# Seven-product blocks in the first layer, another order of blocks, and shifted due times in a planned attention and two-layer kernel

## The chip, the core and the metric

The kernel runs on one core of a Trainium2 chip. Five engines work side by side: PE (TensorE, matrix products), PEld (its weight loads, which overlap PE), DVE (VectorE), ACT (ScalarE), POOL (GpSimd), and SP, whose queue issues all DMAs. The metric is the device time of one execution in microseconds; less is better. What a measurement of this kernel can tell from no change is about 0.2%, some 2.2 us.

## The reference

Attention over 4 batches, 8 heads, 768 positions and 64 columns, with a mask of global and local keys and a bias by distance; its output, 3072 tokens of 512 columns, goes through two layers one after the other.

```
scores = scale * q @ k.T + bias ; masked by keep
a = exp(scores - max) ; a = a / (sum(a) + 1e-9)
x = a @ v                       # 3072 tokens x 512
h = x @ w_in ; g = h * cos(h) ; y = g @ w_out            # first layer, d_ff = 2048
h = max(y @ w_in2, 0) ; out = (h * h) @ w_out2           # second layer
```

## The kernel before

**Blocks.** The tokens are cut into 24 tiles T of 128, and these into six blocks of 512 tokens. Attention runs by tile, in two groups of four heads (`attend`, `group`; `attend32` and `group32` for the first four tiles). Each block then passes through the first layer (m = 0) and the second layer (m = 1). The list SEQ gives the order of these twelve stages.

**Numbers in two parts.** A matrix product in full precision is made as three products of fp16 parts: each operand is split into a high part (an ACT copy) and a low part (a subtraction, `split_lo`, on DVE or on POOL). A unit of the first layer (`first`, 128 hidden columns) is 12 matmuls of 512 columns into one bank of PSUM; `hidden` computes g from it (two ACT steps, a DVE step on line 1099, and a split), and three units later `second` makes another 12 matmuls of 512 columns.

**Weights.** They come as 64-bit numbers. `decoded` turns a pair of rows into fp32 with one ACT step (line 56) and three DVE steps (lines 62, 65, 68), and `weight` splits the result. Sixteen pairs serve the first layer. The tiles w_0 to w_7 keep the eight of the first product; the others go to `ld` tiles, and from there to DRAM and back for each block. The sixteen decodings, the attention of block 0 and that of block 1 all lie ahead of the first layer of block 0 or beside it: this stretch is called the ramp here.

**Seven products.** A product of two 2 x 2 block matrices can be made from seven block products in place of eight. The second layer does its first half so in all six blocks (`four_blocks`, matmuls of 256 columns on line 1166), and its second half so in the blocks named by TWO (`second2`, line 1302); other blocks use `tokens` (line 1372, 512 columns). The code for seven products in the first layer is there too (`four_sums`, `quarters_of_pair`, `four_blocks1`, `second_quarter`), for the blocks named by SEVEN, which is empty.

**Order.** Nothing is issued in the order written. Each step is added to `Plan` with a due time, the engines that may run it and its duration as the planner assumes it; `Plan.order` walks through time and, engine by engine, gives the free engine the ready step with the earliest due time. POOL takes a split when DVE is busy. Buffers come from small pools (4 banks `h`, 4 banks `yp`, 8 tiles `t`, 3 tiles `v`, 2 tiles `e`, 2 `dec`, 2 `raw`). The due times come from `nominal` (attention) and `unit_due` (units and weights).

**Lengths.** `lengths_of_x` runs 16 small matmuls (line 1499) for each block, for a check of the largest argument of the cosine.

## Time and profile before

| | us |
|---|---|
| median of 3 runs | 1114.02 (1113.53 to 1114.48) |
| the profiled execution, device time | 1113.74 |
| its span in the trace | 1112.0 |
| PE busy | 1077.9 |
| DVE busy | 738.1 |
| ACT busy | 734.9 |
| POOL busy | 159.2 |

The trace is of one execution, 0.28 us under the median; its span leaves 1.74 us outside. A matmul's modelled length overlaps the next one's, so the cadence of matmuls is read from start to start, or as a full window divided by its count. A group of matmuls that follow each other without a gap is one row of the timeline.

### The profile page before, as it was taken

Reading aid. Unit: us, or ns where it says so; the run is one execution under the profiler, and the core shown is the slowest. Engines: PE = TensorE matmul, PEld = TensorE weight load, DVE = VectorE, ACT = ScalarE, POOL = GpSimd, SP = SyncE. Lnnn points to the kernel's source line nnn. Section 1 sums busy time; section 2 is a strip of 40 time slices with the busy share of each in tenths; the row PEclk is TensorE's granted clock in tenths of the full one; section 3 lists DMA queues with packets and bytes.
Section 4 is the critical chain, followed back from the end, with each engine's and each line's share of the span. In section 5 each row is a group of like instructions: output and inputs, shape, how many; then the busy total and the mean of one; then the engine's idle time right before and its main releaser. Section 6 shows DMA issues by size and latency. Waiting matters only on the chain.

```text
span 1112.0 us, 21314 instructions
## 1 busy us (share of the span) xinstructions
PE 1077.9 (97%) x8612; PEld 676.5 (61%) x8612; DVE 738.1 (66%) x1341; ACT 734.9 (66%) x1279; POOL 159.2 (14%) x131
## 2 busy tenths in 40 slices
PE   6898889999999999999999999999999999999997
PEld 5744445554455444666666554666544588888886
DVE  6998996668877895675544563455684278477473
ACT  7988867788987664866654865674554277367360
POOL 0210322121130110110000110000140033023010
PEclk9989989999999999999999999999999999999999
DMA  5578778649779773786876624586874363334201
GB/s 218 192 218 209 240 241 251 167 101 274 219 164 226 307 256 127 246 256 211 258 201 221 188 80 94 143 222 187 334 255 148 112 230 131 126 132 153 86 2 42
DMA packets 151979, 207.65 MB, mean 187 GB/s; under 512 B 103808, under 2 KB 104320, under 8 KB 150336
## 3 DMA queue, kind: packets, MB, share of 16 engines
q1 hardware_dynamic: 151872, 206.21, 60.3%
q8 instruction: 69, 1.13, 0.4%
q14 instruction: 38, 0.31, 0.1%
HBM read 149.03 MB, written 32.51 MB: 163 GB/s over the span
## 4 chain that ended last, share of the span: by engine, by line
PE 93%; DVE 5%; ACT 1%; DMA 1%; issue 0%; SPq 0%; DVEq 0%; ACTq 0%
PE hps L1059 22%; PE ypps L1075 22%; PE hps L1166 20%; PE ypps L1372 11%; PE ypps L1302 8%; PE hps L925 2%; PE hps L864 2%; PE hps L1302 2%; PE ypps L761 1%; DVE dec L65 1%; PE hps L879 1%; PE hps L733 1%; PE hps L1499 1%; PE hps L813 1%; DVE dec L68 1%; DMA ld<-kq 1%
## 5 line engine op out<-in xcount | busy, mean ns | idle before, releaser
L1059 PE MATMUL hps<-xy,w 128*128 128x512 f16 x1152 | 269.7, 386 | 9.2 <-DVE w L422 4.8
L1075 PE MATMUL ypps<-g,ld 128*128 128x512 f16 x1152 | 263.7, 379 | 0.4 <-issue 0.4
L1166 PEld LDWEIGHTS <-ld 128*128 128x128 f16 x2016 | 196.2, 98 | 32.3 <-issue 0.7
L1059 PEld LDWEIGHTS <-w 128*128 128x128 f16 x1152 | 111.8, 99 | 144.7 <-issue 11.7
L1166 PE MATMUL hps<-ys,ld 128*128 128x256 f16 x1680 | 196.1, 273 | 0.0
L1075 PEld LDWEIGHTS <-ld 128*128 128x128 f16 x1152 | 111.4, 98 | 131.2 <-issue 0.7
L422 DVE TENSOR_TENSOR g<-t,g 128x512 f16<-128x512 f32 x138 | 103.2, 748 | 53.5 <-ACT g L1143 52.9
L1360 DVE TENSOR_TENSOR t<-hps,t 128x512 f32<-128x512 f32 x120 | 82.7, 689 | 83.6 <-PE hps L1166 82.2
L1372 PE MATMUL ypps<-ld,g 128*128 128x512 f16 x576 | 133.7, 379 | 0.0
L1099 DVE SCALAR_TENSOR_TENSOR t<-t,hps 128x512 f32<-128x512 f32 x96 | 65.6, 684 | 83.8 <-ACT t L1097 83.7
L1095 ACT ACTIVATE t<-hps 128x512 f32<-128x512 f32 x96 | 57.0, 594 | 88.1 <-PE hps L1059 85.4
L1143 ACT ACTIVATE g<-t 128x512 f16<-128x512 f32 x144 | 90.0, 625 | 35.8 <-DVE t L1099 34.5
L1372 PEld LDWEIGHTS <-g 128*128 128x128 f16 x576 | 55.7, 98 | 57.0
L1357 ACT ACTIVATE t<-t 128x512 f32<-128x512 f32 x72 | 45.0, 625 | 55.9 <-DVE t L1360 55.8
L422 POOL TENSOR_TENSOR p<-e,p 128x1024 f16<-128x1024 f32 (+1 forms) x14 | 28.2, 2015 | 239.6 <-ACT p L912 207.6
L1097 ACT ACTIVATE t<-t 128x512 f32<-128x512 f32 x96 | 60.4, 629 | 2.6
L1192 ACT ACTIVATE t<-t 128x512 f32<-128x512 f32 x96 | 60.2, 628 | 2.6
L1357 ACT ACTIVATE t<-hps 128x512 f32<-128x512 f32 x24 | 14.3, 595 | 52.8 <-PE hps L1166 52.8
L888 DVE CUSTOM_DVE_ANT_0 e<-hps,bias 128x256 f32<-128x256 f32 (+2 forms) x96 | 31.7, 386 | 21.0 <-PE hps L864 20.7
L65 DVE SCALAR_TENSOR_TENSOR dec<-raw,dec 128x1024 int32<-128x1024 int32 x32 | 43.7, 1367 | 0.6
L422 DVE TENSOR_TENSOR p<-e,p 128x1024 f16<-128x1024 f32 (+1 forms) x26 | 30.2, 1160 | 20.6 <-ACT p L912 18.9
L422 POOL TENSOR_TENSOR g<-t,g 128x512 f16<-128x512 f32 x18 | 23.2, 1292 | 138.3 <-ACT g L1143 112.7
(195 smaller groups left out, 1527.1 us busy)
## 6 DMA issues: line engine op xcount, KB each, us to landing
ld<-w SPq DMA_DIRECT2D x146, 512.0 KB, 4.2
raw<-w SPq DMA_DIRECT2D x32, 1024.0 KB, 5.5
w<-ld SPq DMA_DIRECT2D x36, 512.0 KB, 3.3
ld<-kq SPq DMA_DIRECT2D x23, 512.0 KB, 5.6
ld<-vt SPq DMA_DIRECT2D x24, 256.0 KB, 4.3
yd<-xy SPq DMA_DIRECT2D x6, 1024.0 KB, 5.8
xy<-yd SPq DMA_DIRECT2D x6, 1024.0 KB, 5.7
ld<-w SPq DMA_DIRECT2D x24, 256.0 KB, 3.7
```

Of the source, the lines that this page charges most:

```text
L422: op.emit = lambda: eng[op.eng].tensor_tensor(out=out_f(), in0=src_f(), in1=hi_f(), op=ALU.subtract)
L1059: nc.tensor.matmul(out=at(ps), lhsT=w_view(wt)[:, a, j % 2, k * 128:(k + 1) * 128], rhs=x_view(src)[:, c, k, :], start=(n == 0), stop=(n = ...
L1075: nc.tensor.matmul(out=at(y_ps[d]), lhsT=wv[:, a, d * 128:(d + 1) * 128], rhs=at(g)[:, c], start=(j == 0 and n == 0), stop=(j == NJ - 1 an ...
L1097: act(due + 1.2, 512, lambda: nc.scalar.activation(out=at(t), in_=at(t), func=ACTF.Square, scale=HALF_TURN), w=[t])
L1099: dve(due + 1.9, 0.7, lambda: nc.vector.scalar_tensor_tensor(out=at(t), in0=at(t), scalar=-S_X / S_H, in1=at(ps), op0=ALU.add, op1=ALU.mul ...
L1143: act(due, 512, lambda: nc.scalar.activation(out=at(g)[:, 0], in_=at(t), func=ACTF.Copy), r=[t], new=[g])
L1166: nc.tensor.matmul(out=at(bank)[:, 256 * u:256 * u + 256], lhsT=wv(a, u, kk), rhs=sv(c, kk), start=(fresh and u == n == 0), stop=(last and ...
L1192: act(due, 512, lambda: nc.scalar.activation(out=at(t), in_=at(t), func=ACTF.Square), w=[t])
L1302: nc.tensor.matmul(out=at(bank)[:, 256 * half:256 * half + 256], lhsT=gv(home)[:, z, c0:c0 + 128], rhs=wv(a, u), start=(q == half == u == ...
L1357: act(due, 512, lambda: nc.scalar.activation(out=at(t), in_=at(ps), func=ACTF.Relu, scale=ROOT), **k)
L1360: dve(due, 0.7, lambda: nc.vector.tensor_tensor(out=at(t), in0=at(bank), in1=at(u), op=ALU.add), port=False, **k)
L1372: nc.tensor.matmul(out=at(y_ps[d]), lhsT=at(g)[:, z, 256 * u + d % 2 * 128:256 * u + d % 2 * 128 + 128], rhs=wv[:, a, u], start=(q == i == ...
```

## The change

The stages stand in another order (block 5's first layer ahead of block 2's second), and block 5's attention is due 30 us sooner. Blocks 4 and 5 now use seven products in the first layer, and block 2 joins the blocks with seven products in the last half of the second layer. The matmuls of `lengths_of_x` are kept for blocks 0 and 1; for the others an ACT square with a running sum takes their place. The due times of attention steps ("P", "A", "X" with the tile) and of the first layer's weights ("W") are shifted by a table of 43 numbers. Where the planner sees PE idle before 240 us of its own time, `idle_products` and `spin` put matmuls of a zero tile on PE. Some temporary tiles come from other pools (`e` for `dec`, `t` for `v`).

```diff
+SHIFTS = {
+    ('A', 0, 0): 7.9,
...
+    ('W', 1, 7): -24.7,
...
+EARLY = 30.0
...
+SPIN_FROM = 0.9
+SPIN_PART = 0.75
+SPIN_UNTIL = 240.0
...
     def order(self):
 
+        for o in self.work:
+            o.due += SHIFTS.get(o.tag, 0.0)
...
-    SEQ = [(0, 0), (0, 1), (0, 2), (0, 3), (1, 0), (1, 1), (0, 4), (1, 2), (0, 5), (1, 3), (1, 4), (1, 5)]
+    SEQ = [(0, 0), (0, 1), (0, 2), (0, 3), (1, 0), (1, 1), (0, 4), (0, 5), (1, 2), (1, 3), (1, 4), (1, 5)]
...
+        if b == NB - 1:
+            s0, s1 = s0 - EARLY, s1 - EARLY
...
-    SEVEN = ()
+    SEVEN = (4, 5)
...
-        if b in SEVEN:
+        if b > 1:
             sq = new("t")
             measured.append(act(s + 24, 600, lambda: nc.scalar.activation(
                 out=at(sq), in_=at(x32), func=ACTF.Square, accum_out=norms[:, T:T + 1]), r=[x32], new=[sq]))
+        if b in SEVEN:
             pair.append(x32)
...
-    TWO = (3, 4, 5)
+    TWO = (2, 3, 4, 5)
...
-        up, low = new("dec"), new("dec")
+        up, low = new("e"), new("e")
...
-            tiles[b, n] = tuple(new("v") for _ in range(3))
+            tiles[b, n] = tuple(new("t" if (b, n) == (TWO[-1], 1) else "v") for _ in range(3))
...
-        if m == 0 and b not in SEVEN:
+        if m == 0 and b < 2:
             lengths_of_x(b, start[0, b] + 6)
...
+            if last is not None and o.start < SPIN_UNTIL and biased[0].end < o.start:
+                gap = o.start - last.end
+                open_y = [y for y in sums.values() if y[1].end <= last.end]
+                if gap > SPIN_FROM:
...
+                    n = int(SPIN_PART * (o.start - begin) / 0.216)
+                    if bank is not None and n > 0:
+                        out[o] = bank, n, not open_y
...
+    def spin(bank, n, fresh):
+
+        for _ in range(n):
+            nc.tensor.matmul(
+                out=at(bank), lhsT=nought, rhs=bias.rearrange("p h c -> p (h c)")[:, 0:512], start=fresh, stop=fresh,
+                skip_group_check=True)
+
     order = plan.order()
+    idle = idle_products(order)
     with tc.manual_schedule():
         for o in order:
+            if o in idle:
+                spin(*idle[o])
             o.emit()
```

**First place: DVE in the ramp, up to the split of w_4**, the weight tile that the ninth unit needs. raw and dec are the tiles of a weight that is being decoded, x_1 and g_125 belong to attention's output, nm to attention's row maxima, t and hps to a unit's `hidden`. Before:

```order
L65 SCALAR_TENSOR_TENSOR dec_105<-raw_64,dec_105 128x1024
L68 SCALAR_TENSOR_TENSOR dec_105<-raw_64,dec_105 128x1024
L62 TENSOR_SCALAR dec_104<-dec_104 128x1024
L941 RECIPROCAL sm_93<-sm_93 128x4
L942 TENSOR_TENSOR x_1_123<-hps_133,sm_93 128x2x128
L65 SCALAR_TENSOR_TENSOR dec_104<-raw_63,dec_104 128x1024
L820 TENSOR_REDUCE nm_87<-hps_135 128x2
L820 TENSOR_REDUCE nm_87<-hps_136 128x2
L824 TENSOR_SCALAR nm_87<-nm_87 128x4
L422 TENSOR_TENSOR g_125<-x_1_123,g_125 128x512
L68 SCALAR_TENSOR_TENSOR dec_104<-raw_63,dec_104 128x1024
L422 TENSOR_TENSOR w_4_110<-dec_105,w_4_110 128x1024
```

After, the same place:

```order
L62 TENSOR_SCALAR dec_105<-dec_105 128x1024
L65 SCALAR_TENSOR_TENSOR dec_105<-raw_64,dec_105 128x1024
L1165 SCALAR_TENSOR_TENSOR t_116<-t_116,hps_136 128x512
L68 SCALAR_TENSOR_TENSOR dec_105<-raw_64,dec_105 128x1024
L1165 SCALAR_TENSOR_TENSOR t_117<-t_117,hps_135 128x512
L703 SCALAR_TENSOR_TENSOR v_82<-ld_70,v_82 128x8x64
L474 TENSOR_TENSOR w_4_110<-dec_105,w_4_110 128x1024
```

Attention's maxima and the next weight's steps no longer stand between w_4's decoding and its split: 147 instructions stand ahead of that split before, 128 now (and one of these is a new memset). The sixteenth unit's step on line 1099 (1165 now) has 208 ahead of it before and 206 now.

**Second place: DVE just ahead of the first unit**, whose operand is the split of xy_101 into xy_102. Before:

```order
L422 TENSOR_TENSOR p_97<-e_95,p_97 128x1024
L65 SCALAR_TENSOR_TENSOR dec_105<-raw_64,dec_105 128x1024
L68 SCALAR_TENSOR_TENSOR dec_105<-raw_64,dec_105 128x1024
L422 TENSOR_TENSOR ld_69<-dec_104,ld_69 128x1024
L422 TENSOR_TENSOR xy_102<-xy_101,xy_102 128x1024 x2
```

After:

```order
L474 TENSOR_TENSOR ld_72<-dec_105,ld_72 128x1024
L68 SCALAR_TENSOR_TENSOR dec_104<-raw_63,dec_104 128x1024
L703 SCALAR_TENSOR_TENSOR v_83<-ld_67,v_83 128x8x64
L474 TENSOR_TENSOR xy_102<-xy_101,xy_102 128x1024
L878 TENSOR_REDUCE nm_88<-hps_133 128x2
L878 TENSOR_REDUCE nm_88<-hps_134 128x2
```

One half of the operand's split stays on DVE and the other moves to POOL, and a third attention group's maxima (nm_88) follow at once.

**Third place: DVE in the second layer of block 1**, where a bank of PSUM is freed by the sums on line 1360 (1426 now). Before:

```order
L1360 TENSOR_TENSOR t_118<-hps_135,t_119 128x512
L1360 TENSOR_TENSOR t_119<-hps_134,t_119 128x512
L422 TENSOR_TENSOR g_125<-t_118,g_125 128x512
L941 RECIPROCAL sm_91<-sm_91 128x4
L942 TENSOR_TENSOR x_0_122<-hps_133,sm_91 128x2x128
L1360 TENSOR_TENSOR t_115<-hps_134,t_115 128x512
```

After:

```order
L1426 TENSOR_TENSOR t_121<-hps_136,t_121 128x512
L474 TENSOR_TENSOR g_128<-t_117,g_128 128x512
L631 TENSOR_TENSOR t_114<-dec_104,dec_105 128x512
L631 TENSOR_TENSOR dec_105<-dec_105 128x2x256
L474 TENSOR_TENSOR g_124<-t_118,g_124 128x512
L631 TENSOR_TENSOR t_115<-dec_105,dec_104 128x512
L474 TENSOR_TENSOR g_127<-t_121,g_127 128x512
L1426 TENSOR_TENSOR t_117<-hps_135,t_117 128x512
L652 TENSOR_TENSOR dec_104<-w_3_109 128x1024
```

The sums of weights for the first layer's seven products (`four_sums`, lines 631 and 652) now stand between the sums that free PE's banks. In all, the planned path has 1442 DVE instructions for 1341 before, 62 more on ACT and 62 more on POOL; of the sums on line 1360 there are 160 for 120.

## Rows read from the trace of the kernel before

**Rows 1.** The page: span, part 1 (busy time), PEclk of part 2.

```profile
span 1112.0 us, 21314 instructions
PE 1077.9 (97%) x8612; PEld 676.5 (61%) x8612; DVE 738.1 (66%) x1341; ACT 734.9 (66%) x1279; POOL 159.2 (14%) x131
PEclk9989989999999999999999999999999999999999
```

**Rows 2.** Waits of PE: waiter, releaser, total us, times, longest.

```profile
PE hps L1059 <- DVE w L422: 4.8, 2, 3.0
PE hps L813 <- ACT e L828: 4.7, 2, 2.5
...
PE hps L1059 <- DVE dec L68: 1.9, 1, 1.9
...
PE hps L1166 <- DVE t L1360: 0.5, 1, 0.5
```

**Rows 3.** Timeline of PE, ramp: start, length, instruction, count, idle before and releaser.

```profile
59.56 4.41 PE L1059 MATMUL hps<-xy,w 128*128 128x512 f16 x11 [0.97 <-DVE xy L422]
63.80 1.06 PE L1499 MATMUL hps<-xy 128*128 128x128 f16 x16
64.69 2.75 PE L1059 MATMUL hps<-xy,w 128*128 128x512 f16 x12
67.28 0.89 PE L925 MATMUL hps<-v,pt 128*128 128x65 f16 x24
...
109.22 4.92 PE L1059 MATMUL hps<-xy,w 128*128 128x512 f16 x22 [3.04 <-DVE w L422]
...
126.73 0.38 PE L813 MATMUL hps<-bias,ident 128*128 128x448 bf16 x2 [2.54 <-ACT e L828]
...
127.81 4.45 PE L1059 MATMUL hps<-xy,w 128*128 128x512 f16 x12
...
138.27 0.90 PE L925 MATMUL hps<-v,pt 128*128 128x65 f16 x24 [0.83 <-DMA pt<-p]
141.05 0.60 PE L1059 MATMUL hps<-xy,w 128*128 128x512 f16 x2 [1.88 <-DVE dec L68]
143.39 7.53 PE L1059 MATMUL hps<-xy,w 128*128 128x512 f16 x22 [1.73 <-DVE w L422]
```

**Rows 4.** Windows: stretch, length, busy PE, PEld, DVE, ACT, POOL, clock, DMA.

```profile
60.00:160.00 100.00, 89.97 (x675) 43.87 (x674) 89.29 (x115) 81.90 (x125) 20.96 (x12) 0.93 0.78 233
...
450.00:620.00 170.00, 170.00 (x1475) 113.11 (x1473) 97.78 (x224) 109.89 (x193) 15.01 (x9) 1.00 0.76 230
...
1000.00:1040.00 40.00, 40.00 (x369) 35.85 (x367) 24.87 (x51) 21.74 (x42) 10.61 (x11) 1.00 0.32 107
```

**Rows 5.** Timeline of DVE and POOL, at 59 and at 119 us.

```profile
59.42 1.22 DVE L422 TENSOR_TENSOR xy<-xy,xy 128x1024 f16<-128x1024 f32 x1
...
119.23 2.13 POOL L422 TENSOR_TENSOR w<-dec,w 128x1024 f16<-128x1024 f32 x1
119.39 3.05 DVE L65 SCALAR_TENSOR_TENSOR dec<-raw,dec 128x1024 int32<-128x1024 int32 x1
```

**Rows 6.** Groups by line: shapes, count, busy us, mean ns, idle before.

```profile
L1360 DVE TENSOR_TENSOR t<-hps,t 128x512 f32<-128x512 f32 x120 | 82.7, 689 | 83.6 <-PE hps L1166 82.2
L1328 DVE SCALAR_TENSOR_TENSOR v<-ypps,v 128x256 f32<-128x256 f32 x35 | 13.3, 419 | 33.5 <-ACT v L1337 28.1 <-PE ypps L1302 5.3
L1192 ACT ACTIVATE t<-t 128x512 f32<-128x512 f32 x96 | 60.2, 628 | 2.6
```

**Rows 7.** One line's durations, min/median/max in ns, first and last start.

```profile
L65 DVE SCALAR_TENSOR_TENSOR dec<-raw,dec x32: 1210/1225/3050, 24.2 to 475.3; 128x1024 int32<-128x1024 int32 x32
L1360 DVE TENSOR_TENSOR t<-hps,t x120: 675/692/692, 450.9 to 1079.9; 128x512 f32<-128x512 f32 x120
```

**Rows 8.** Timeline of the last 12 us.

```profile
1099.96 4.75 PE L1302 MATMUL hps<-w,e 128*128 128x256 f16 x42
...
1103.21 2.75 DVE L1328 SCALAR_TENSOR_TENSOR v<-hps,v 128x256 f32<-128x256 f32 x7 [1.83 <-DMA out<-v]
```

More of the change, by code (lines that the diff above doesn't have):

```diff
@@ L83 @@
 PASSING = 10
+SHIFTS = {
+    ('A', 0, 0): 7.9,
+    ('A', 0, 1): -2.2,
+    ('A', 1, 0): -4.4,
+    ('A', 1, 1): -2.2,
+    ('A', 2, 0): -2.2,
+    ('A', 2, 1): -2.2,
+    ('A', 3, 0): -2.2,
+    ('A', 3, 1): -2.2,
+    ('A', 4, 0): -2.2,
+    ('A', 4, 1): 4.2,
+    ('A', 5, 0): -2.2,
+    ('A', 5, 1): -19.1,
+    ('A', 6, 0): -2.2,
+    ('A', 6, 1): -2.2,
+    ('A', 7, 0): -6.5,
+    ('A', 7, 1): -8.6,
+    ('A', 8, 0): -2.2,
+    ('A', 8, 1): -2.2,
+    ('A', 9, 0): -2.2,
+    ('A', 9, 1): 1.7,
+    ('P', 1): -1.8,
+    ('P', 2): 7.8,
+    ('P', 4): -21.4,
+    ('P', 6): 9.8,
+    ('P', 9): -13.4,
+    ('W', 0, 0): -18.2,
+    ('W', 0, 1): -18.2,
+    ('W', 0, 2): -30.9,
+    ('W', 0, 3): -19.4,
+    ('W', 0, 4): -16.1,
+    ('W', 0, 5): -18.2,
+    ('W', 0, 6): -18.2,
+    ('W', 0, 7): -18.2,
+    ('W', 1, 0): -18.2,
+    ('W', 1, 1): -12.2,
+    ('W', 1, 2): -18.2,
+    ('W', 1, 3): -13.1,
+    ('W', 1, 4): -18.2,
+    ('W', 1, 5): -12.7,
+    ('W', 1, 6): -18.2,
+    ('W', 1, 7): -24.7,
+    ('X', 7): -17.9,
+    ('X', 8): 3.7,
+}
+EARLY = 30.0
 ROUNDS = 1
+SPIN_FROM = 0.9
+SPIN_PART = 0.75
+SPIN_UNTIL = 240.0
 class Buf:
@@ L92 @@
 class Work:
-    __slots__ = ("ways", "due", "emit", "deps", "gets", "bufs", "start", "end", "eng", "left", "outs", "n", "lag", "tab")
+    __slots__ = ("ways", "due", "emit", "deps", "gets", "bufs", "start", "end", "eng", "left", "outs", "n", "lag", "tab", "tag")
     def __init__(self, ways, due, emit):
@@ L102, in __init__ @@
         self.free = {k: list(range(n)) for k, n in pools.items()}
-        self.work, self.row = [], []
+        self.work, self.row, self.tag = [], [], None
     def add(self, ways, due, emit, r=(), w=(), new=(), part=(), after=(), lag=0.1, tab=None):
         o = Work(ways, due, emit)
-        o.lag, o.tab = lag, tab
+        o.lag, o.tab, o.tag = lag, tab, self.tag
         for b in new:
@@ L402, in fast_path @@
     ident32 = const.tile([128, 128], FP32, name="ident32")
+    nought = const.tile([128, 128], BF16, name="nought")
     norms = const.tile([128, NT + NJ // 4], FP32, name="norms")
@@ L1012, in attend @@
     def attend(T):
+        plan.tag = "P", T
         prepare(T)
@@ L1647, in fast_path, with idle_products @@
     farthest(start[0, 5] + 30)
+    def idle_products(order):
+        out, last, before, busy, sums = {}, None, {}, {}, {}
+        for o in order:
+            for b in o.gets:
+                before[b] = busy.get((b.pool, b.slot), 0.0)
+            for b in o.bufs:
+                if b.slot is not None:
+                    busy[b.pool, b.slot] = max(busy.get((b.pool, b.slot), 0.0), o.end)
+        for o in order:
+            if o.eng != "PE":
+                continue
+            if last is not None and o.start < SPIN_UNTIL and biased[0].end < o.start:
+                gap = o.start - last.end
+                open_y = [y for y in sums.values() if y[1].end <= last.end]
+                if gap > SPIN_FROM:
+                    own_b = [b for b in o.gets if b.pool in banks and b.writers[0] is o]
+                    bank, begin = None, last.end
+                    if open_y:
+                        bank = open_y[-1][0]
+                    elif own_b:
+                        bank, begin = own_b[0], max(begin, before[own_b[0]] + 0.3)
+                    n = int(SPIN_PART * (o.start - begin) / 0.216)
+                    if bank is not None and n > 0:
+                        out[o] = bank, n, not open_y
+            for y in (b for bs in y_all for b in bs if b in o.bufs):
+                if o is y.writers[-1]:
+                    sums.pop(y, None)
+                elif o is y.writers[0]:
+                    sums[y] = y, o
+            last = o
+        return out
+    def spin(bank, n, fresh):
[3 more added lines that the diff above has]
+                skip_group_check=True)
     order = plan.order()
+    idle = idle_products(order)
     with tc.manual_schedule():
         for o in order:
+            if o in idle:
+                spin(*idle[o])
             o.emit()
```

19 lines of the change are left out of this document (16 added, 3 removed).

## The prediction, made before the changed kernel had run

> **What bounds the kernel now.** I read the page's busy times first: PE is busy 97% of a span of 1112.0 us, DVE and ACT 66% each, POOL 14% [rows 1]. So the end is PE's work plus the time in which PE stands or runs slowly. The clock row (PEclk) says where the second part is: it falls to 8 in the slices from 56 and from 139 us and is 9 in every one behind. Next, what PE waits for: DVE's split and decoding of weights on the line of the first layer's units, and ACT's exponentials in attention; behind the ramp there is one wait of 0.5 us for the sums on line 1360 [rows 2]. Then PE's timeline in the ramp, for the place and the price of each wait [rows 3], and three windows, to see which engine has room there [rows 4]: from 60 to 160 us DVE is busy 89.3 of 100, so DVE sets the pace of the ramp; from 450 to 620 us, the second layer of blocks 0 and 1, PE is busy all 170 and DVE 97.8. Most of the kernel is thus PE's own work, and what takes matmuls away comes off one for one; the ramp is DVE's, and there the order on DVE counts.
>
> **Cadences.** Twelve matmuls of 512 columns start at 64.69 and what follows them at 67.28: 2.59 us, 215.8 ns each [rows 3]. In the window from 1000 us, in which all matmuls have 256 columns, 369 take 40.00 us: 108.4 ns each [rows 4]. The sixteen matmuls of lengths start at 63.80 and their successor at 64.69: 0.89 us [rows 3].
>
> **Part 1, seven products in the first layer of blocks 4 and 5.** The first product has 16 units of 12 matmuls in a block, 384 in two blocks: 384 x 215.8 ns = 82.9 us. In their place come 336 of 256 columns in each: 672 x 108.4 ns = 72.8. That is -10.0 us. The second product keeps its columns but in halves: 384 of 512 columns (82.9) become 768 of 256 (83.3), +0.4.
>
> **Part 2, block 2 in TWO.** Its last product was 192 x 215.8 ns = 41.4 and is now 336 x 108.4 ns = 36.4: -5.0 us.
>
> **Part 3, lengths.** Four of six blocks lose their 16 small matmuls: 4 x 0.89 = -3.6 us. Sixteen squares on ACT replace them, of the shape of ACT's line 1192 (0.628 us each [rows 6]): 10 us on an engine busy 734.9 of 1112.0 [rows 1], counted at nothing. If that cover were gone they would cost 0.63 us each where PE waits for x.
> Parts 1 to 3 make -10.0 + 0.4 - 5.0 - 3.6 = -18.2 us, all while PE has no gap.
>
> **Part 4, the ramp.** What can be won is limited by what is lost. After the first unit PE stands 3.04 + 2.54 + 0.83 + 1.88 + 1.73 = 10.0 us [rows 3]. Slow matmuls add: the first unit's eleven take 4.24 us from start to next start, where full speed gives 2.4 (1.9 lost); the twelve at 127.81 show 4.45 for the 2.75 of twelve at 64.69 (1.7); the twenty-two at 143.39 show 7.53 for the 4.92 of those at 109.22 (2.6). Together 16.2 us; the granted clock of the stretch is 0.93 [rows 4], and the slow pieces come right behind pauses. The releasers are weights made on DVE. The change moves them earlier in DVE's order: the split of w_4 has 128 instructions ahead of it instead of 147. But the last unit's hidden step has 206 instead of 208, and these two, together with moved shapes, come by the rows' mean durations to some 2 us less. So DVE's work in the ramp is nearly the same, and only its sequence is better. Lower end: DVE's idle time stays and PE gains 2.0. Upper end: DVE's 10.7 us of idle time (100 - 89.3) go too, because PE no longer holds it up: 12.7. No row is nearer to one end, so I take the middle, -7.5 us.
> Inside this part, half of the first operand's split goes from DVE (1.22 us) to POOL (2.13 us for a split of that shape) [rows 5]: it starts sooner and lasts longer, taken at 0, between -1 and +1. The three attention maxima that now stand right behind it delay no unit that PE has reached.
>
> **Part 5, idle products.** 32 matmuls of 512 columns are 32 x 215.8 ns = 6.9 us. 25 stand ahead of the first unit and 7 behind it, all in time that the planner holds for idle. They are taken at 0; where PE would not have stood, they cost up to 6.9. What they may save is the slow matmuls, inside the 16.2.
>
> **Part 6, new waits behind the ramp.** Seven products need sums of weights (`four_sums`) and quarters. By the order DVE has 101 instructions more and POOL 62 more; 40 are sums on line 1360, 40 x 0.689 = 27.6 us, and 14 are on line 1328, 14 x 0.419 = 5.9 us [rows 6], beside the last products. In the second layer of block 1 the sums of weights now stand between the sums that free PE's banks: about eight recombinations, five of them on POOL, and with their combining and splits about 17 us on DVE and 31 on POOL, worked out from the rows of the nearest shapes (0.69 for 512 columns, 1.2 on DVE and 2.1 on POOL for 1024). DVE comes to 97.8 + 17 = 115 of 170, 68%; POOL to 15.0 + 31 = 46. A wait here holds one bank of four: behind a sum, two splits and a combining can queue, about 3 us, while PE has some 3.5 us of matmuls in the other banks. How much of that shows, no row tells. At 58% it was 0.5 us for the line [rows 2], at 89%, in the ramp, 10.0 us. Bounds 0 and 9 us; nearer in load to the first, so +3.
>
> **Part 7, the tail.** One of the last sums waits 1.83 us for a DMA to give back its tile, while PE's last 42 matmuls run until 1104.7 [rows 8]. The tiles of that row now come from a pool that no DMA holds. What is late next is PE's own last bank, so most of the wait was covered: -0.5 (0 to -1).
>
> **A rule weighed.** The decoding step that started at 119.39, 0.16 us behind a split on POOL, took 3.05 us instead of 1.23 [rows 5, 7]: it ended 1.1 us behind POOL's, as if it had begun when POOL was done. The sums on line 1360, with one operand in PSUM, keep to 675 to 692 ns in all 120 cases [rows 7]. The Trainium skill ("SBUF — State Buffer", Who interferes with whom) has it so: a DVE instruction with two inputs in SBUF and one of GpSimd that reads SBUF lock each other out for the whole instruction, and one with a single SBUF input does not. By that rule the bank-freeing sums go on beside POOL and part 6 grows only by what queues ahead of them; the trace agrees in both rows.
>
> **Sum.** 1113.74 - 18.2 - 7.5 + 3 - 0.5 = 1090.5 us against the profiled execution. The median of the runs is 0.28 higher: 1090.8, so 1091.
>
> **Rivals.**
> A, the ramp stays DVE's. For it: DVE was 89% busy there [rows 4] and its work is only 2 us less, so weights that come sooner push attention later, and ACT's exponentials (4.7 us of PE's waits [rows 2]) become the wait. Then part 4 is -2.0: 1096; with idle products that stand in PE's way, about 1097 to 1100. This is also the case in which the new order doesn't do what it says.
> B, the ramp clears and nothing new waits. Part 4 is -12.7 and part 6 is 0: 1113.74 + 0.28 - 18.2 - 12.7 - 0.5 = 1082.6. For it: every wait in the ramp is of an order that can be shifted. Against: DVE would have to be 100% busy there.
> C, DVE and POOL shut each other out. If each POOL instruction of parts 4 and 6 stops DVE for its length, as at 119 us [rows 5], DVE in the second layer of blocks 0 and 1 has 97.8 + 15.0 + 48 = 161 of 170 us [rows 4], 48 being the 17 and 31 of part 6. At 95% it is loaded like the ramp, which stood 10.0 us in 100; over 170 us that is up to 17, and as only block 1's half has the sums, I price it at 9 to 14 in place of 3: 1097 to 1102. Against it: the sums on line 1360 never grew, and POOL had 15.0 us in the same stretch.
> D, slower than before: block 5 comes late. Its first layer now follows block 4's at once, with no second layer (some 80 us of matmuls, four quarters of 84 x 108.4 ns and a last product of 36 to 41 us) between, while its attention was moved by 30 us alone. By the order and the mean durations, DVE is through with that attention some 30 us of its own work ahead; of that 10 go to the last transposes, splits and sums of quarters, so about 20 are slack. Any delay beyond it stops PE one for one. The kernel is slower than before from 23 us beyond that slack, a delay of 43 us in all; at 60 us it would be 1131. For it: DVE has 101 instructions more in all. Against: behind the ramp DVE is at 58 to 62% [rows 4], with room to catch up.
>
> **Chances.** The forecast, 1085 to 1095: 0.62. A: 0.15. B: 0.12. C: 0.08. D: 0.03, most of it slower. A measurement of this kernel can tell 0.2%, some 2.2 us, from no change; all but D and its edge lie more than 10 us below. So faster 0.95, same 0.02, slower 0.03. The range takes the bounds of parts 4 and 6: from B's 1082.6 with a shorter x split and tail, 1081, to C's 1102. Beyond lie D and the worst of A, some 0.06, and what I have not thought of.
>
> **What would show it.** Parts 1 and 2: in the groups by line, 672 more matmuls of 256 columns on the line of `four_blocks` and its first-layer twin, 192 fewer of 512 in the last products, PE's busy time down by 15 to 19 us. Part 3: 32 small length matmuls left instead of 96. Part 4: in PE's waits the 4.8 and 1.9 us on DVE's weights fall under 3 together, and no slice behind the first unit shows an 8. Part 5: spins end before the unit's operand is there; if a unit's operand is done while spins still run, they cost. Part 6: waits of the second layer's matmuls for line 1360 (1426 then) come to 1 to 6 us; with over 9, rival C, above all where POOL's and DVE's rows grow beside each other. Part 7: the last sums without a DMA as releaser. D: a pause of PE of many us where block 5's first layer begins. The prediction is wrong if PE's matmuls fall by less than 15 us of work, or if new waits behind the ramp take more than the ramp returns.

## The result and the profile after

The changed kernel takes 1094.22 us (median of four, 1092.40 to 1094.64), the kernel before 1113.78 beside it: a ratio of 0.9821, with a 95% interval of 0.9804 to 0.9838. The forecast was 1091 with a range of 1081 to 1102, so the time lies in the range, 3 us above the point. The profiled execution has a device time of 1094.64. The ratios here and below are worked out over all executions of both kernels and not from the two medians, so they can differ from the medians' quotient by up to 0.001.

From the page of the changed kernel, the answers to [rows 1]:

```profile
span 1092.9 us, 23235 instructions
PE 1064.8 (97%) x9396; PEld 755.3 (69%) x9396; DVE 802.4 (73%) x1442; ACT 750.9 (69%) x1349; POOL 247.8 (23%) x193
PEclk9999999999999999999999999999999999999998
```

PE is still busy 97% of the span, but the span is shorter. DVE has gone from 66% to 73% and POOL from 14% to 23%. The two slices of the clock row that showed an 8 in the ramp are gone; the last 8 lies behind the last matmul.

What PE waits for in the changed kernel, the answer to [rows 2] (waiter, releaser, total us, times, longest):

```profile
...
PE hps L1232 <- DVE t L1426: 2.3, 3, 1.3
PE hps L871 <- ACT e L886: 2.2, 3, 1.1
PE ypps L1183 <- DVE flag_i L1791: 1.8, 1, 1.8
PE ypps L1141 <- DVE g L474: 1.6, 1, 1.6
PE hps L1125 <- DVE x L1000: 1.2, 1, 1.2
...
PE ypps L1183 <- DVE g L474: 0.5, 1, 0.5
...
```

The waits of 4.8 and 1.9 us for DVE's weights are gone from the list. The waits for the sums that free banks (line 1426, 1360 before) have grown from 0.5 to 2.3 us. New are one of 1.8 us for a flag (0.4 at that place before), which the prediction had not named, one of 1.6 us at 140 us for a split, and one of 1.2 us at 192 us for attention's x.

Windows of the changed kernel, as [rows 4] (stretch, length, busy PE, PEld, DVE, ACT, POOL, clock, DMA):

```profile
60.00:160.00 100.00, 97.33 (x736) 48.45 (x734) 94.86 (x122) 84.33 (x133) 30.60 (x17) 1.00 0.85 252
450.00:620.00 170.00, 168.40 (x1531) 113.49 (x1529) 125.93 (x270) 124.02 (x233) 56.06 (x33) 0.99 0.85 245
516.00:526.00 10.00, 8.40 (x49) 4.50 (x47) 9.89 (x45) 8.24 (x20) 0.00 (x0) 0.83 0.59 231
```

In the ramp PE is busy 97.3 of 100 us where it was 90.0, and the granted clock is 1.00 where it was 0.93. In the second layer of blocks 0 and 1 it is the other way round: 168.4 of 170 where it was 170.0, and in the ten microseconds from 516 the clock is 0.83.

To compare the kernels by terms I used one sum throughout: for each matmul, the time from its start to the next matmul's start; what its shape takes at full speed is work, what is above it is loss, and the idle products are counted apart. It is worked out from all matmul starts of the two traces.

| us | before | changed | difference |
|---|---|---|---|
| work of PE | 1024.5 | 1007.6 | -16.9 |
| loss up to 160 us, idle products included | 48.3 | 37.4 | -10.9 |
| loss behind 160 us | 24.5 | 31.8 | +7.3 |
| from the last matmul's start to the end | 7.6 | 8.8 | +1.2 |

With 0.2 us at the very start this makes the 19.1 us between the two spans. The levels depend on the price that is put on attention's short matmuls; with other prices the differences move by less than 1 us.

### The profile page after: what moved, and what is told of

Same layout as the page of the kernel before. It is cut to its first block, busy times and chain, and to the rows that moved or that the text cites. A ratio compares the mean times of both kernels' runs of the same rounds, so it can differ in the third digit from the quotient of the medians.

```text
span 1092.9 us, 23235 instructions
## 1 busy us (share of the span) xinstructions
PE 1064.8 (97%) x9396; PEld 755.3 (69%) x9396; DVE 802.4 (73%) x1442; ACT 750.9 (69%) x1349; POOL 247.8 (23%) x193
## 4 chain that ended last, share of the span: by engine, by line
PE 85%; DVE 9%; ACT 4%; issue 1%; DMA 0%; SPq 0%; DVEq 0%; ACTq 0%
PE hps L1232 25%; PE ypps L1141 13%; PE hps L1125 13%; PE ypps L1368 11%; PE ypps L1183 7%; PE ypps L1438 7%; PE hps L983 2%; PE hps L1368 2%; PE hps L922 2%; PE hps L788 1%; DVE dec L65 1%; DVE nm L878 1%; PE hps L937 1%; PE hps L871 1%; DVE dec L68 1%
## 5 line engine op out<-in xcount | busy, mean ns | idle before, releaser
L1232 PEld LDWEIGHTS <-ld 128*128 128x128 f16 x2400 | 234.5, 98 | 35.7 <-issue 2.6
L1141 PE MATMUL ypps<-g,ld 128*128 128x512 f16 x768 | 175.8, 379 | 1.6 <-DVE g L474 1.6
L1125 PE MATMUL hps<-xy,w 128*128 128x512 f16 x768 | 174.3, 379 | 1.2 <-DVE x L1000 1.2
L1426 DVE TENSOR_TENSOR t<-hps,t 128x512 f32<-128x512 f32 x160 | 110.0, 688 | 68.8 <-PE hps L1232 65.8
L1141 PEld LDWEIGHTS <-ld 128*128 128x128 f16 x768 | 74.0, 98 | 88.7 <-POOL g L474 1.9
L1125 PEld LDWEIGHTS <-w 128*128 128x128 f16 x768 | 73.7, 98 | 87.7 <-DVE x L1000 1.7
L474 DVE TENSOR_TENSOR g<-t,g 128x512 f16<-128x512 f32 (+1 forms) x129 | 99.6, 777 | 29.9 <-ACT g L1209 29.4
L1183 PE MATMUL ypps<-g,ld 128*128 128x256 f16 x768 | 89.2, 273 | 2.3 <-DVE flag_i L1791 1.8
L1438 PE MATMUL ypps<-ld,g 128*128 128x512 f16 x384 | 90.1, 381 | 0.0
L1183 PEld LDWEIGHTS <-ld 128*128 128x128 f16 x768 | 75.0, 98 | 11.5 <-issue 2.7
L1423 ACT ACTIVATE t<-t 128x512 f32<-128x512 f32 x72 | 45.0, 624 | 48.3 <-DVE t L1426 48.0
L1161 ACT ACTIVATE t<-hps 128x512 f32<-128x512 f32 x72 | 42.6, 592 | 30.2 <-PE hps L1125 20.8
L474 POOL TENSOR_TENSOR g<-t,g 128x512 f16<-128x512 f32 (+1 forms) x23 | 28.8, 1251 | 142.2 <-ACT g L1209 134.8
```

The lines of the kernel that those rows point to most:

```text
L474: op.emit = lambda: eng[op.eng].tensor_tensor(out=out_f(), in0=src_f(), in1=hi_f(), op=ALU.subtract)
L1125: nc.tensor.matmul(out=at(ps), lhsT=w_view(wt)[:, a, j % 2, k * 128:(k + 1) * 128], rhs=x_view(src)[:, c, k, :], start=(n == 0), stop=(n = ...
L1141: nc.tensor.matmul(out=at(y_ps[d]), lhsT=wv[:, a, d * 128:(d + 1) * 128], rhs=at(g)[:, c], start=(j == 0 and n == 0), stop=(j == NJ - 1 an ...
L1183: nc.tensor.matmul(out=at(y_ps[d])[:, 256 * n:256 * n + 256], lhsT=w_view(wt)[:, a, u, d * 128:(d + 1) * 128], rhs=at(g)[:, z, 256 * u:256 ...
L1232: nc.tensor.matmul(out=at(bank)[:, 256 * u:256 * u + 256], lhsT=wv(a, u, kk), rhs=sv(c, kk), start=(fresh and u == n == 0), stop=(last and ...
L1426: dve(due, 0.7, lambda: nc.vector.tensor_tensor(out=at(t), in0=at(bank), in1=at(u), op=ALU.add), port=False, **k)
```

## The experiments

All ratios are against the kernel before, run on the same chip with the kernel in question.

### The idle products

The changed kernel with one number changed:

```
-SPIN_UNTIL = 240.0
+SPIN_UNTIL = 0.0
```

> The changed kernel without its 32 idle products; the order of everything else is the same. Theory S (idle products pay through TensorE's clock): in the changed kernel no half-speed stretch lies between 20 and 500 us, while the kernel before has three, 20.5 us in all. Without the idle products the granted clock falls to 0.5 again about the first unit (near 60 us) for some 10 us, and near 135 us; the time rises by 3 to 6 us, to 1097 to 1100. Theory N (they cost nothing and save nothing, as the sum of the prediction had it): 1094, within 1.5. Theory D (they stand in the way: the thirteen before the first unit end at 61.24, while DVE's half of its operand was done at 60.25): 1 to 2 us faster, 1092 to 1093, with the first unit starting at about 60.3.

Measured: 1096.0 us, ratio 0.9819 (0.9806 to 0.9831), the changed kernel's own ratio. Theory S falls. PE's timeline without idle products, at the first unit:

```profile
58.10 0.29 PE L937 MATMUL hps<-kq,kq 64*128 64x96 f16 x6
59.00 0.38 PE L1125 MATMUL hps<-xy,w 128*128 128x512 f16 x1 [0.61 <-ACT xy L860]
60.26 1.45 PE L1125 MATMUL hps<-xy,w 128*128 128x512 f16 x6 [0.88 <-DVE xy L474]
62.25 1.24 PE L1125 MATMUL hps<-xy,w 128*128 128x512 f16 x5 [0.54 <-POOL xy L474]
```

And with them, in the changed kernel:

```profile
58.42 2.98 PE L1754 MATMUL hps<-bias,nought 128*128 128x512 bf16 x13
61.24 2.75 PE L1125 MATMUL hps<-xy,w 128*128 128x512 f16 x12
```

Without them the unit starts 2.2 us sooner, at 59.00, but stops again for DVE's half of the operand and then for POOL's; with them it starts late, runs through, and is done about 0.3 us later. Without them half-speed stretches stand at 51 and at 140 us, but of 3.4 us each, not the 20.5 us of the kernel before: the new order has already taken away the long pauses. The one at 51 us follows a pause of 1.02 us, in which the changed kernel has three idle products. The one at 140 us is no evidence for the idle products. It follows a pause of 1.60 us that is there with them too, and it also stands in the changed kernel's second trace (the same program once more, below) and in three further traces below (all sums on POOL, both fixes, block 2's last product), all with the idle products. The loss up to 160 us is 38.4 us without them and 37.4 with them; in the changed kernel's second trace it is as large as in the one without them. Within the spread of the executions they save what they cost.

### The products alone, the ramp alone

Products only: the table of shifts is not applied, and there are no idle products.

```
-            o.due += SHIFTS.get(o.tag, 0.0)
+            o.due += 0.0
...
-SPIN_UNTIL = 240.0
+SPIN_UNTIL = 0.0
```

> The changed kernel with an empty table of shifts and no idle products: the seven products, the lengths, the buffers and the order of blocks alone. By the terms of the prediction it is 18.2 faster than before less 3 of new waits and 0.5 of tail: 1098. Theory W (read from the two traces: matmuls of 256 columns come at 109.2 ns, so the work falls by 16.9; the waits behind 160 us grow by 7; the tail grows by 1): 1113.8 - 16.9 + 7 + 1 = 1105, the ramp as before with three half-speed stretches. Rival A of the prediction (the ramp gives only 2, all the rest comes from the products): 1096.

Measured: 1105.09 us, ratio 0.9918 (0.9904 to 0.9932), as theory W had it; -9.1 us. Its times lie wide, from 1102.5 to 1108.1, and the trace is of the lowest. In it the loss up to 160 us is 48.3 us, the same as before to the tenth, and the work is 1007.6.

Ramp only: the shifts and the idle products, everything else as before except the tiles of the last sums, which come from the new pool.

```
-    SEQ = [(0, 0), (0, 1), (0, 2), (0, 3), (1, 0), (1, 1), (0, 4), (0, 5), (1, 2), (1, 3), (1, 4), (1, 5)]
+    SEQ = [(0, 0), (0, 1), (0, 2), (0, 3), (1, 0), (1, 1), (0, 4), (1, 2), (0, 5), (1, 3), (1, 4), (1, 5)]
...
-EARLY = 30.0
+EARLY = 0.0
...
-    SEVEN = (4, 5)
+    SEVEN = ()
...
-    TWO = (2, 3, 4, 5)
+    TWO = (3, 4, 5)
...
-        if m == 0 and b < 2:
+        if m == 0 and b not in SEVEN:
```

> The kernel before with the table of shifts and the idle products alone (no seven products added, old order of blocks, old lengths, block 5's attention not sooner). By the prediction's ramp term: 7.5 faster, 1106. By the two traces (loss of PE up to 160 us is 48.3 before and 37.2 after): 11 faster, 1103. Rival A (ramp stays DVE's): 2 faster, 1112. If the shifts only pay together with the new order of blocks, it is 1112 or slower.

Measured: 1112.25 us, ratio 0.9978 (0.9969 to 0.9987). Only 2.5 us came, where 7.5 (the forecast's term) or 11 (the two traces) were expected. It is the time that was expected of rival A, and of shifts that pay only together with the new order of blocks. Two rows of its trace, PE's timeline and the window of the ramp:

```profile
73.94 1.01 PE L1141 MATMUL ypps<-g,ld 128*128 128x512 f16 x2 [4.26 <-DVE g L474]
```

```profile
60.00:160.00 100.00, 94.94 (x683) 47.35 (x682) 91.07 (x112) 80.04 (x126) 32.62 (x16) 0.97 0.81 227
```

The same table gives another ramp here, with a new wait of 4.26 us. The order of DVE's instructions is that of the changed kernel for 81 instructions of the two traces and then parts from it. The reason is in the planner. When it chooses for DVE it asks whether POOL has something to do and is free; if so, a two-input step on DVE is put back by 12 us (`BESIDE`). The sums of weights for blocks 4 and 5 may run on POOL and are ready as soon as a pair is decoded, though they are due hundreds of us later. So with seven products POOL's list is never empty, and the choice on DVE is another one in the ramp. An edit of one line takes this over without the products:

```
     def waits_for_pool(self, ready, free_at, now):
-        return free_at["POOL"] <= now + 1e-9 and any(i[2].eng is None for i in ready["POOL"])
+        return free_at["POOL"] <= now + 1e-9
```

> As ramp_only, the kernel before with the table of shifts and the idle products, but with one more edit in the planner: when it chooses for DVE it always counts POOL as having something to do. In the changed kernel the sums of weights for blocks 4 and 5 are ready as soon as the first pair is decoded and stand in POOL's list for hundreds of us; the planner then puts 12 us on each DVE step with two inputs whenever POOL is free, and by that DVE's order in the ramp is another one from its 83rd instruction on. With this edit DVE's first 254 instructions stand as in the changed kernel, and there are the same 32 idle products. Theory O (the ramp's gain is a matter of this order alone): PE's loss up to 160 us falls from 48.3 to 37 or 38 us, and the time by 10 to 11, to a ratio of 0.990 to 0.991. Rival (the ramp's gain needs the products too): about 0.998, as ramp_only.

Measured: 1103.34 us, ratio 0.9902 (0.9887 to 0.9917): theory O. The window of its ramp:

```profile
60.00:160.00 100.00, 97.32 (x749) 48.57 (x748) 94.86 (x121) 84.02 (x132) 30.32 (x17) 1.00 0.83 253
```

That is the changed kernel's row to 0.01 us of PE. Its loss up to 160 us is 37.6. This kernel has the old order of blocks, so the ramp's gain does not need the new one. With the right order the two halves add up: -9.1 from the products and -10.9 from the ramp make the -20 of both.

### What the seven products of blocks 4 and 5 bring

```
-    SEVEN = (4, 5)
+    SEVEN = ()
```

With it goes the planner line above, so that the ramp keeps its order.

> The changed kernel without seven products in the first layer of blocks 4 and 5 (block 2 keeps its seven in the second layer's last product), with the same planner edit as ramp_order, so that DVE's first 400 instructions stand as in the changed kernel. By the cadences, PE's work grows by 9.5 (first product, 672 matmuls of 256 at 109.2 ns against 384 of 512 at 215.8) less 1.0 (second product in halves): +8.5. Theory W (the sums of weights cost PE waits of 2.2 us at 517 to 520, a half-speed stretch of 3.4 us behind them, and 0.9 at 640): these go too, and the kernel is 4 to 5 slower than the changed one, ratio 0.986. Rival (the sums cost nothing): 8.5 slower, ratio 0.990.

Measured: 1095.24 us, ratio 0.9832 (0.9819 to 0.9846), 1 us above the changed kernel; the intervals overlap. Both expectations were too high: the rival has no waits at all, and theory W has neither the flag's wait nor the longer end. In its trace the work is 8.6 us more, as the cadences say, but the loss behind 160 us is 25.0 for 31.8, and the end comes 7.4 us after the last matmul's start and not 8.8. So of the 8.6 us of matmuls saved, 6.8 are paid for in waits and slow stretches and 1.4 behind the last matmul. Of the 6.8, 1.7 is the half-speed stretch at 520 us, which does not come in every execution (last section); between their lowest executions, 1095.15 and 1092.40 us, the two kernels lie 2.8 us apart. The wait for line 1426 that is left in it:

```profile
PE hps L1232 <- DVE t L1426: 1.0, 2, 0.5
```

The waits at 517 to 520, at 640 and for the flag are gone with the seven products.

### The sums of weights and the port

In the changed kernel DVE and POOL stand like this ahead of the wait that ends at 520 us (timeline of DVE, POOL and PE, each in order of time):

```profile
505.96 1.59 POOL L631 TENSOR_TENSOR t<-dec,dec 128x512 f32<-128x512 f32 x1 [0.69 <-DVE g L474]
507.63 1.60 POOL L631 TENSOR_TENSOR dec<-dec 128x512 f32<-128x512 f32 x1
509.31 2.13 POOL L631 TENSOR_TENSOR t<-dec,dec 128x512 f32<-128x512 f32 x1
...
513.22 2.44 POOL L652 TENSOR_TENSOR dec<-w 128x1024 f32<-128x1024 f16 x1
```

```profile
506.34 1.75 DVE L474 TENSOR_TENSOR ys<-t,ys 128x512 f16<-128x512 f32 x1
508.02 2.29 DVE L474 TENSOR_TENSOR kq<-ld,kq 128x1024 f16<-128x1024 f32 x1
510.24 1.49 DVE L474 TENSOR_TENSOR g<-t,g 128x256 f16<-128x256 f32 x1
...
512.38 1.30 DVE L474 TENSOR_TENSOR g<-t,g 128x512 f16<-128x512 f32 x1
513.61 2.60 DVE L474 TENSOR_TENSOR ys<-xy,ys 128x512 f16<-128x512 f32 x1
```

```profile
520.06 2.58 PE L1232 MATMUL hps<-ys,ld 128*128 128x256 f16 x12 [1.31 <-DVE t L1426]
```

The five splits take 9.4 us. Each ends 0.3 to 1.1 us behind a POOL instruction, about as if it had begun when that one was done (alone these shapes take 0.41 to 1.21 us, below). Behind PE's pause twelve matmuls of 256 columns show 2.58 us, where 1.47 is usual, and the clock of the window is 0.83 (above). To find out whether it is the lock or the amount of work, the 13 of the 24 adding steps that run on POOL were put on DVE, in the same place of the order (`plan.tag = "S"` is set while a block's sums are planned):

```
     idle = idle_products(order)
+    for o in order:
+        if o.tag == "S":
+            o.eng = "DVE"
```

> The changed kernel in its own order, but the 13 of the 24 adding steps of the sums of weights that run on POOL run on DVE, at the same place in the order; nothing else moves. Theory L (DVE and POOL shut each other out): between 506 and 516 us five splits on DVE took 9.4 us beside POOL's sums and would take 3.7 alone; the sums cost DVE 0.4 to 1.2 us each, some 4.0 for those five. So DVE is 1 to 2 us earlier at 517 us, PE's wait of 1.31 there falls below 0.5, the half-speed stretch at 520 us goes, and the time falls by 1 to 3, ratio 0.979 to 0.981. Rival Q (DVE simply has too much to do there): DVE's list grows by 4 us, the wait grows to 3 or more, ratio 0.984 to 0.986.

Measured: 1092.14 us, ratio 0.9801 (0.9787 to 0.9814). The same splits in its trace, one of the adding steps, and the window of PE's old wait:

```profile
505.98 0.68 DVE L474 TENSOR_TENSOR ys<-t,ys 128x512 f16<-128x512 f32 x1
506.58 1.21 DVE L474 TENSOR_TENSOR kq<-ld,kq 128x1024 f16<-128x1024 f32 x1
507.72 0.41 DVE L474 TENSOR_TENSOR g<-t,g 128x256 f16<-128x256 f32 x1
...
513.50 0.69 DVE L631 TENSOR_TENSOR t<-dec,dec 128x512 f32<-128x512 f32 x1
```

```profile
516.00:526.00 10.00, 10.00 (x75) 6.25 (x74) 9.96 (x31) 9.06 (x19) 0.00 (x0) 1.00 0.43 167
```

1.75, 2.29 and 1.49 have become 0.68, 1.21 and 0.41, PE does not stop there, and the clock stays at 1.00. DVE does five more steps and is earlier. A wait of 1.07 us comes up at 560 instead, where DVE's list is now longer. Theory L, as far as the splits and the pause go. The time is less clear: most of the 1 to 2 us is the half-speed stretch that does not follow here, and with the pause still in place it stays away in some traces too (last section). The lowest executions are 1092.40 us for the changed kernel and 1091.75 here.

The opposite edit, all 24 on POOL (`o.eng = "POOL"`):

> The opposite: the other 11 adding steps, which run on DVE in the changed kernel, run on POOL at the same place in the order; all 24 are there then. Theory L: each adds 1.6 to 2.4 us in which DVE's two-input steps in SBUF stand, and the sums for a bank that follow them are late: PE's waits for line 1426 grow from 2.3 to 5 us or more, ratio 0.984 to 0.988. Rival Q: DVE is relieved by 11 steps of 0.4 to 1.2 us, the wait at 517 us shrinks or goes, ratio 0.980.

Measured: 1094.20 us, ratio 0.9817 (0.9803 to 0.9830): no change, which neither theory expected. The wait at 520 is the same, and one of 0.95 us for a split on DVE is added at 537:

```profile
521.48 1.47 PE L1234 MATMUL hps<-ys,ld 128*128 128x256 f16 x12 [1.31 <-DVE t L1428]
...
537.22 2.55 PE L1440 MATMUL ypps<-ld,g 128*128 128x512 f16 x11 [0.95 <-DVE g L474]
```

Here the twelve matmuls after the pause of 1.31 us show 1.47: in this execution the clock did not fall behind that pause, but behind the one at 140 us. So what the new wait costs, about 1.1 us, can be hidden by the spread of the executions: the lowest here took 1093.92 us, the changed kernel's 1092.40. The other steps moved to POOL made PE wait nowhere; why just these were covered was not tried, and the test tells the two theories apart no further.

### The wait for the flag

All engines load a flag into a register before they go on. In the changed kernel, PE's timeline there:

```profile
733.29 0.60 PE L1591 MATMUL hps<-ident,longest 128*1 128x128 f32 x4
733.83 1.48 PE L1232 MATMUL hps<-xy,w 128*128 128x256 f16 x12
737.15 2.78 PE L1183 MATMUL ypps<-g,ld 128*128 128x256 f16 x24 [1.84 <-DVE flag_i L1791]
```

First the flag's computation was planned as a step of its own, ahead of the load (`pre` below; the load is `due + 60`):

```
-        plan.add((("DVE", 2.0, False),), due + 60, lambda: meanwhile(reach[:, 2:3]), after=[o])
+        pre = plan.add((("DVE", 1.5, False),), due + 50, lambda: meanwhile(reach[:, 2:3], False), after=[o])
+        plan.add((("DVE", 0.6, False),), due + 60, lambda: meanwhile(reach[:, 2:3], True), after=[pre])
```

> The changed kernel with one edit: the range flag is computed on DVE ten planned microseconds sooner, and the engines' load of it stays where it was. In the changed kernel PE stands 1.84 us at 735 us for that flag; the kernel before has 0.37 at the same place in its program. Theory F (PE stands because the flag's chain of small DVE steps begins only when PE has reached the load): the wait falls to 0.5 or less and the time by 1.3 to 1.8 us, to 1092.5. Rival (the load itself empties PE's queue, whatever the flag's time): the wait stays at 1.5 to 2 us, and so does the time, 1094.

Measured: 1093.75 us, ratio 0.9806 (0.9793 to 0.9819). The wait is 1.1 us, between the two theories; the time alone tells nothing here. The next kernel has the sums on DVE and the flag's computation at `due + 60` again, with the load at `due + 140`, 24 matmuls further down:

> sums_on_dve with one more edit: the engines' load of the range flag stands some 24 matmuls later in PE's order, the flag's computation stays. In the changed kernel twelve matmuls of 256 columns (1.3 us) lie on PE between the product that starts the flag's chain and its load, where the kernel before has twelve of 512 (2.6 us), and the chain takes 3.3 us; so PE stands 1.84 us. Theory F2 (the wait is the cover that is missing): with 24 more matmuls between, it is gone, and the time falls by 1.8 against sums_on_dve, to a ratio of 0.978 to 0.979, 3 to 4 us below the changed kernel. Rival (the load itself drains PE): a wait of 1 us or more stays at the new place, ratio 0.980.

Beside it the changed kernel ran once more:

> The changed kernel once more, beside the next two on the same chip: 1094, ratio 0.981 to 0.983. In its executions the half-speed stretch of 3.4 us at 520 us comes or stays away, which is 1.7 us.

Measured: 1094.15 us, ratio 0.9810 (0.9795 to 0.9825), and both fixes 1091.18 us, ratio 0.9789 (0.9776 to 0.9802). The wait was still 1.11 us, as the rival had it. POOL and DVE in that kernel:

```profile
734.14 2.12 POOL L1283 TENSOR_TENSOR e<-ld 128x1024 f32<-128x1024 f16 x1
```

```profile
734.23 2.03 DVE L1602 TENSOR_TENSOR reach<-reach 1x1 f32<-1x1 f32 x1
```

In the changed kernel the same product of two single numbers stands as:

```profile
735.47 0.15 DVE L1600 TENSOR_TENSOR reach<-reach 1x1 f32<-1x1 f32 x1
```

There POOL stood at the load and disturbed nobody; here it works on, and one number takes 2.03 us, until POOL is done. In the test with the early flag the same product took 2.04 us beside such a sum, which is why 1.1 us stayed there too. Last, the load 156 matmuls further down, by hand in the finished order:

```
+    at_load = next(i for i, o in enumerate(order) if o.tag == "F")
+    order.insert(at_load + 60, order.pop(at_load))
```

> both_fixes with the load of the flag moved 156 matmuls (17 us) further down PE's order; nothing else moves. In both_fixes the wait was still 1.11 us, because the flag's chain grew: its product of two single numbers took 2.03 us in place of 0.15 while POOL was in a sum of 2.12 us that the load had held back before. Theory F3 (the wait is cover that is missing, and the chain's length depends on POOL): PE no longer stands at the load, the time falls by 1.3 against both_fixes, ratio 0.977 to 0.978, 1090. Rival (the load itself drains PE): 0.5 to 1.1 us stay at the new place, ratio 0.979.

Measured: 1090.59 us, ratio 0.9787 (0.9774 to 0.9801). PE no longer waits for the flag; its list of waits now has

```profile
...
PE hps L873 <- ACT e L888: 3.3, 3, 2.1
PE hps L1234 <- DVE t L1428: 2.0, 3, 1.1
PE ypps L1143 <- DVE g L474: 1.6, 1, 1.6
...
```

with no line for the flag, and the loss behind 160 us is 27.4 us, 4.4 less than in the changed kernel, of which 1.7 is the stretch at 520 us. So the load does not drain PE; the wait was cover that was missing. Against both fixes the time is 0.6 us lower, which the intervals don't separate; against the changed kernel's 1094.2 the two edits together give about 3.6 (2.6 between the lowest executions), and this is the fastest version here.

### Block 2's last product

```
-    TWO = (2, 3, 4, 5)
+    TWO = (3, 4, 5)
```

> The changed kernel with block 2's last product made of eight products again, as before. By the cadences PE's work grows by 192 x 215.8 ns less 336 x 109.2 ns = 4.7 us: ratio 0.986, the waits unchanged. Rival (seven products bring as many waits here as in the first layer): ratio 0.982, no change.

Measured: 1097.15 us, ratio 0.9839 (0.9826 to 0.9853), 3.0 above the changed kernel beside it. The work grows by 4.8 us, as the cadence says; a wait of 0.6 at 896 us goes, and the end follows the last matmul's start by 7.7 us in place of 9.0. So here about 3 of 4.8 us arrive.

## Why the prediction was right, and where its terms were off

**Parts 1 to 3, -18.2 forecast, -16.9 found.** The count of matmuls was right, the price of 256 columns wrong. I divided a window of 40.00 us by the 369 matmuls listed in it [rows 4] and got 108.4 ns. That window also counts the matmuls that reach over its edges. From start to start it is more. The changed kernel's last products:

```profile
1075.08 4.75 PE L1368 MATMUL ypps<-w,g 128*128 128x256 f16 x42
1079.67 4.75 PE L1368 MATMUL hps<-w,e 128*128 128x256 f16 x42
```

42 matmuls in 4.59 us are 109.3 ns, and over all such pairs it is 109.2. With that, the first product gives -9.5, the second +1.0, block 2's last product -4.7, the lengths -3.6: -16.8. The row that would have told it stood in the trace of before as well: 42 matmuls from 1095.38 to 1099.96. PE's busy time fell by 13.1 us, less than the 15 to 19 I had named for it. The 6.9 us of idle products are inside it, which I had left out there; without them it fell by 20.0, which fits that matmuls at half speed count as busy too and became fewer. On the line of the length matmuls 96 are left of 160 and not 32 of 96, because the line serves the weights too; the 64 fewer are as counted.

**Parts 4 and 5, -7.5 forecast, -10.9 found.** The mechanism held: the waits for weights went, the slow stretches with them, and DVE's order did it, as the ramp with the order alone shows. The term that was mis-sized is DVE's idle time, of which I took half as recoverable (the middle of 2.0 and 12.7 is 7.35). Between DVE's step for the first unit (line 1099, now 1165) and its step for the sixteenth, the idle time fell from 10.9 to 3.4 us: 7.5 of it went, about 70%. DVE's work up to the sixteenth step is 1.5 us less (142.2 for 143.7), near the 2 that I had, and that step comes 8.9 us sooner. (In the fixed window DVE went from 89.3 to 94.9 of 100, which looks like half, but the changed kernel has later work in that window.) About 1 us more was won ahead of 58 us, which I had not counted. So the gain came near the upper end of 12.7. Where the long pauses went, the matmuls behind them ran at full speed too: the granted clock of the stretch is 1.00 for 0.93. In the changed kernel's second trace a half-speed stretch stands at 140 us, and the gain is 1.4 us less. The idle products cost and save about the same, so 0 was right for them, for another reason than the one I gave: not all of them lay in idle time. Rival A is out; PE is busy 97.3 of 100 in the ramp. Of rival B the ramp came nearly true, but not that nothing new waits.

**Part 6, +3 forecast, +7.3 found.** The waits for line 1426 come to 2.3 us, close to the 3 I had, but not where I put them, in the second layer of block 1. The longest, 1.31 us, ends at 520 us, near the end of block 0's second layer, where the sums of weights have begun; the others, of 0.48 and 0.46 us, stand at 897 and 971 us in the second layers of blocks 3 and 4, and the kernel before has one of 0.48 at 991. So 1.8 us of the 2.3 are new. In the second layer of blocks 0 and 1 DVE came to 125.9 of 170 us and POOL to 56.1, where I had 115 and 46. What I left out are three other things. The pause at 520 us can have a half-speed stretch behind it, 3.4 us long in this trace, which costs 1.7. The flag's wait grew from 0.37 to 1.84 us, because the twelve matmuls that cover it have 256 columns now and not 512: 1.3 us of cover in place of 2.6. And 1.25 us come at 192 us, where attention's x is late for a unit of block 1; they belong to the new ramp, since they stand in its trace without the products too. The rest is a wait of 0.46 us for a split at 640. These make some 6.7 of the 7.3 us. I had looked for new waits by asking which engine gets more to do, and not where PE's own matmuls, which become shorter, hide something.

**Rival C** was the right mechanism with too high a price. The lock is there, in rows, at 506 to 516 us, and taking it away moved the time by 1 to 2 us (a ratio of 0.9801 for 0.9810 and 0.9821, whose intervals overlap; that the wait at 520 us went is shown by the trace), the half-speed stretch included, and not by the 6 to 11 that C asked beyond the forecast. The sums on line 1426 themselves kept their 675 to 693 ns, as [rows 7] had it before. The Trainium skill ("SBUF — State Buffer", Who interferes with whom), that a DVE instruction with two inputs in SBUF and a GpSimd instruction that reads SBUF lock each other out, is borne out by the split of 2.29 us that became 1.21, and by the single number that took 2.03 us in place of 0.15. By that rule part 6 should grow by what queues ahead of the sums, and so it did: the sums don't suffer, the splits ahead of them in DVE's list do, and the sums come late.

**Part 7, -0.5 forecast, +1.2 found.** DVE's wait of 1.83 us for a DMA [rows 8] is gone as forecast; the last rows of DVE in the changed kernel are

```profile
1082.49 0.42 DVE L1394 SCALAR_TENSOR_TENSOR t<-hps,t 128x256 f32<-128x256 f32 x1 [0.47 <-PE hps L1368]
1083.80 1.87 DVE L1394 SCALAR_TENSOR_TENSOR t<-hps,t 128x256 f32<-128x256 f32 x5 [0.89 <-PE hps L1368]
```

and they wait for PE alone. But DVE's last step ends 1.5 us behind the last matmul's start in both kernels, so that wait had been covered whole, and the term was 0. Still the end comes 8.8 us after the last matmul's start and not 7.6. DVE's and SP's last instructions of the program stand as far behind the last matmul as before; what comes later is the closing of SP's queue, where SP stands 1.4 us between two of its closing semaphore steps that follow within 0.1 us in the kernel before. In the trace of each kernel with both sets of seven products this is 8.4 to 9.1 us, in those that lack one or both 7.4 to 8.0, with the new tiles or without. Why it stands there was not tried, and stays open.

**Rival D** did not come: block 5's first layer begins near 714 us, and from 641 us to the flag at 735 us PE has no wait of 0.3 us or more. The 0.46 us at 640 belong to block 4's first layer.

So the time came out near the forecast partly by luck, because misses cancel: the ramp gave 3.4 us more, and the work (1.3), the waits (4.3) and the tail (1.7) took 7.3 more.

## What to carry to other kernels

A saving of matmuls on a PE that is busy all the time is not one for one, if the saving is bought with work on the engines that free its banks: here 8.6 us of matmuls in the first layer returned 1 to 3 us, and about 3 more when the adding steps were put where they don't lock the others out and the flag's load where it is covered. When a matmul gets shorter, look for what stands behind it in the order and was hidden by its length. And a table of preferences that was fitted to one plan is a part of that plan: the same shifts gave 2.5 us with the old list of steps and 11 once the planner chose as it does with the new one, since it chooses by what stands ready elsewhere. Last, when a change is worth 1 or 2 us, look at the clock of each trace before the medians are compared.

## What the runs showed of the hardware

A DVE step on two operands of a single number took 2.03 us beside a POOL sum of 1024 columns that took 2.12 us, and ended with it; without such a sum it took 0.15. So even so small a step stood until POOL's instruction was done.

A short pause of PE can be followed by a stretch of 3.4 us at a granted clock of 0.5 (1.2 GHz), or not. The pause of 1.31 us for line 1426 (at 520 us, at 530 with the products only) stands in seven traces. In four the stretch follows: the changed kernel both times, the one without idle products, and the one with block 2's last product undone. In three it does not: products only, the early flag, and all sums on POOL. Of the eleven traces with the pause of 1.60 us at 140 us, five have the stretch. The changed kernel itself has the one at 520 us in its first trace (1094.64 us) and both in its second (1096.11 us). Windows of the two at 140 us, as [rows 4], first and second:

```profile
139.00:144.00 5.00, 3.81 (x18) 1.76 (x18) 4.81 (x8) 4.96 (x9) 4.31 (x3) 1.00 0.63 216
```

```profile
139.00:144.00 5.00, 4.08 (x12) 1.53 (x12) 4.80 (x8) 4.97 (x9) 4.32 (x3) 0.66 0.66 221
```

So one and the same program takes some 2 us more or less from one execution to the next, which is as much as several of the differences above. What decides it was not found.
